# Two key chunks loaded and turned on their own, the rest by a transposed transfer; folds, pools and double-step plans in another order

## The chip, the core and the metric

The kernel runs on one core of a Trainium2 chip. Its time is the device time of one execution in microseconds (us); the median of several executions is what counts. The core has five engines that run side by side, each with its own instruction stream in a fixed order: TensorE (PE, with weight loads PEld), VectorE (DVE), ScalarE (ACT), GpSimd (POOL) and SyncE (SP), which here issues nearly all transfers. Each waits on semaphores for the others. SBUF is the on-chip memory; PSUM holds what TensorE computes, in eight banks here used in pairs.

## What is computed

The input x has 2048 tokens of 640 numbers (bfloat16); there are 32 heads of 20. Two attention layers A and B work on the same x, and a gate per token mixes them.

```python
# A: linear attention, features are softmax(+p) and softmax(-p) of p = (x W) w_phi
qkv = (x @ wqkv).reshape(B, S, 3, H, Dh) ...
pk = jnp.einsum('bhsd,hdf->bhsf', k, w_phi)
phi_k = jnp.concatenate([_softmax(pk), _softmax(-pk)], axis=-1)
kv = jnp.einsum('bhsf,bhsd->bhfd', phi_k, v);  z = jnp.einsum('bhsf->bhf', phi_k)
o = einsum(phi_q, kv) / (einsum(phi_q, z) + 1e-06);  a = o @ wo
# B: four segments of 512 tokens, causal softmax attention and a memory M, z of earlier segments
p = _softmax(q_s k_s^T * scale + mask);  a_dot = p v_s
a_mem = phi(q_s) M / (phi(q_s) z + 1e-06)
o = sig(beta) * a_mem + (1 - sig(beta)) * a_dot;  M += phi(k_s)^T v_s;  z += sum phi(k_s);  b = o @ wo
# mix
g = sigmoid((x * gate_w).sum(-1));  out = g * a + (1 - g) * b
```

## The kernel before, in words

Nearly every instruction's order is written out by hand, engine by engine; no planner reorders it. So an instruction that waits holds up all that stand behind it on its engine, and a transfer that waits holds up SP's queue.

**Front (L84 to L315).** The key weights of layer A are multiplied by w_phi beforehand (the fold), so that one product gives the features' exponents. The five 128-row blocks of these weights (wnat_k) come in five transfers, blocks 0, 2, 4 issued by ACT (L96), 1 and 3 by SP (L105). A step `T`n (`emit_foldT`, L175) turns block n with five TensorE transposes and copies it out of PSUM (L180, to WkT, on DVE or ACT). A step `M`n (`emit_foldM`, L182) makes six small matmuls of it with Wphi, a masked w_phi that DVE and POOL build (L144), and ACT copies the result to WkA (L190). A step `X`n (`emit_xT`, L192) turns 256 tokens of x, loaded plainly into x_nat (L102), with ten transposes, and DVE copies them to the first quarter of xTf (L200). The order is T0 T1 T2 M0 M1 T3 T4 M2 X0 X1 M3 M4 (L305), behind 25 transposes of ident_b that only warm TensorE up (L304). The other quarters of x, 512 tokens each, come turned by the transfer itself (`emit_xturn`, L113): quarters 1 and 2 right after the loads of the value weights WvA (L110), quarter 3 after chunk 1.

**Key chunks (L224 to L257).** The 2048 tokens are handled in 16 chunks of 128. Chunk sc belongs to quarter sc // 4 and takes every fourth token of it (`key_tokens`, L224, through the view xTk); quarter 3 is first put into runs (xP, L116). `emit_a1` (L229) computes pk (ten matmuls with WkA) and pv (ten with WvA); ACT takes two exponentials of pk and copies pv, DVE sums and takes the reciprocal, POOL multiplies (EkSn). `emit_zmove` (L252) sends EkSn to Z with two transfers on SP. The gate column of WvA is filled from gw (L314, L315).

**Rest of layer A (to L682).** The kv products, the sums over Z, the query features (pq), then for each of 16 query chunks the numerators (`emit_num`, L455, in three PSUM pools nps0 to nps2), the denominators and the divisions (tt, L508 on DVE; oA, L666 on POOL). Between them go half projections (320 columns each) of layer B's first segment, out of the pool pps.

**Layer B (L687 on).** 32 steps (segment and group of four heads) are taken in pairs: 16 double steps. Each makes five bursts: TensorE computes two PSUM tiles of scores (st_ps, L736, pools st_a and st_b), ACT takes their exponentials (PT, L740), POOL cuts the triangles (L747). Between the bursts TensorE gets other work, one letter an item, by a string of PLAN per double step:

- `h` half projection of the next segment (five matmuls, L922; DVE copies them out, L928), `o` and `f` out projections (L866; out by L875 or L877, and then a transfer L879). All use the two buffers of the pool bps.
- `k`, `q` an exponential of a projected chunk on ACT (L894); `x`, `y` the two DVE instructions that finish its features (L897, L898), x for keys and y for queries; `z` the transposed transfer of finished query features (L907).
- `A` and `B` products with the values for the double step's first step and for the step before it (L790), `D` and `C` the last of these with the memory products (L798, L803) and the epilogue on DVE and POOL (L815 to L837).
- `t` turns one output chunk (L841), `u` turns the first three column blocks of the last segment's four chunks (L960).

SHARES holds four numbers per double step: after burst n the items are handed out until that share of the plan's matmul work is done, and after the fifth burst all that is left. An `h`, `o` or `f` counts 0.137 for each matmul of 320 columns; k, q, x, y, z, t and u count nothing, so they fall between their neighbours. The tail (L1000 on) finishes the last step and the last four output chunks, which read the turned blocks of `u` (L1046).

Of the kernel before, what the change touches and what calls it, by code (L numbers as in the profile page):

```python
# [15 lines left out]
def kernel(  # L16
# [35 lines left out]
    xq = xTf[:, S // 4:].rearrange("p (g c t) -> p g c t", g=4, c=KC)  # L52
    beta_b = const.tile([P, H], BF16, name="beta_b")
# [27 lines left out]
    x_nat = []  # L81
# [3 lines left out]
    xv = x2.rearrange("(c p) d -> p c d", p=P)  # L85
# [13 lines left out]
    def emit_xload():  # L99
        x_nat.append(xload.tile([P, 2, D], BF16, name="x_nat"))  # L100
        c0 = 2 * len(x_nat) - 2
        nc.sync.dma_start(out=x_nat[-1], in_=xv[:, c0:c0 + 2, :])  # L102

    for c in (1, 3):
        nc.sync.dma_start(out=wnat_k[:, c], in_=wsrc(D)[:, c])  # L105
    for n in range(2):
        emit_xload()
    nc.sync.dma_start(out=gw5, in_=gate_w.rearrange("(c p) -> c p", p=P))
    for bk in range(2):
        nc.sync.dma_start(out=WvA[:, :, bk, 0:320], in_=wsrc(2 * D)[:, :, bk * 320:(bk + 1) * 320])  # L110
# [71 lines left out]
    def emit_foldM(WT, dst, ic):  # L182
        ps = w2tile("fold_ps")
        for n, (j, bk, lo, hi) in enumerate(PIECES):
            h0 = TH[j][0]
            nc.tensor.matmul(ps[:, bk, (lo - 16 * bk) * DH:(hi - 16 * bk) * DH],
                             lhsT=WT[:, j, ic * P:(ic + 1) * P],
                             rhs=Wphi[:, j, lo - h0:hi - h0, :].rearrange("p h d -> p (h d)"),
                             start=(n in FIRST), stop=(n in LAST))
        nc.scalar.copy(out=dst[:, ic, :].rearrange("p (b n) -> p b n", b=2), in_=ps[:, :, 0:320])  # L190

    def emit_xT(n):  # L192
        pair = w2tile("xtp")
        for u in range(2):
            tp = pair[:, u].bitcast(BF16)[:, 0:D].rearrange("p (c t) -> p c t", c=KC)
            for c in range(KC):
                nc.tensor.transpose(out=tp[:, c, :], in_=x_nat[n][:, u, c * P:(c + 1) * P], identity=ident_b)
# [4 lines left out]
    WkT = wq_hold.tile([P, KC, D], BF16, name="WkT")  # L202

# [18 lines left out]
    xTk = xq.rearrange("p g c (m r) -> p g c r m", r=4)  # L222

    def key_tokens(c, sc):  # L224

        g, r = divmod(sc, 4)
        return xTk[:, g, c, r] if g < 3 else xP[:, c, r * P:(r + 1) * P]

    def emit_a1(sc):  # L229
        pk, pv = w2tile("pk"), w2tile("pv")  # L230
        for ps, W, n in ((pk, WkA, 320), (pv, WvA, 321)):
            by_row = [(c, bk) for c in range(KC) for bk in range(2)]
            for c, bk in by_row if sc == 0 else sorted(by_row, key=lambda t: t[1]):
                rhs = WvA[:, c, bk, :] if W is WvA else WkA[:, c, bk * 320:(bk + 1) * 320]
                nc.tensor.matmul(ps[:, bk, 0:n], lhsT=key_tokens(c, sc), rhs=rhs,  # L235
                                 start=(c == 0), stop=(c == KC - 1))
# [65 lines left out]
    warm = [aps.tile([P, KC, P], BF16, name="warm", tag="w2") for _ in range(2)]  # L302
    for n in range(25):
        nc.tensor.transpose(out=warm[n % 2][:, n % KC, :], in_=ident_b, identity=ident_b)  # L304
    for step in ("T0", "T1", "T2", "M0", "M1", "T3", "T4", "M2", "X0", "X1", "M3", "M4"):  # L305
        n = int(step[1])
        if step[0] == "T":
            emit_foldT(wnat_k, WkT, n, nc.scalar.copy if n in (1, 4) else nc.vector.tensor_copy)
        elif step[0] == "M":
            emit_foldM(WkT, WkA, n)  # L310
        else:
            emit_xT(n)
    gw_ps = aps.tile([P, KC], BF16, name="gw_ps", tag="w2")
    nc.tensor.transpose(out=gw_ps, in_=gw5, identity=ident_b[0:KC, 0:KC])  # L314
    nc.vector.tensor_copy(out=WvA[:, :, :, 320:321],  # L315
                          in_=gw_ps[:, :, None, None].to_broadcast([P, KC, 2, 1]))
    for sc in range(NCH):
        emit_a1(sc)
        emit_zmove(sc)
        if sc == 1:  # L320
            emit_xturn(3)
# [239 lines left out]
    for what in "ppppvzppppdvp":  # L561
# [14 lines left out]
    *nps, pps = [nps_stack.enter_context(tc.tile_pool(  # L576
        name=n, bufs=b, space=bass.MemoryType.PSUM, reuse_waits="tile"))
        for n, b in (("nps0", 1), ("nps1", 1), ("nps2", 1), ("pps", 2))]
# [108 lines left out]
    with ExitStack() as bctx:  # L687
# [5 lines left out]
        bps, st_a, bnd, st_b = [bctx.enter_context(tc.tile_pool(  # L693
            name=n, bufs=b, space=bass.MemoryType.PSUM, reuse_waits="tile"))
            for n, b in (("bps", 2), ("st_a", 1), ("bnd", 1), ("st_b", 1))]
# [239 lines left out]
        def half_items(s, order):  # L935
# [207 lines left out]
```

## Time and profile before

| what | us |
|---|---|
| median of three runs | 320.29 (318.81 to 320.96) |
| the profiled execution | 319.04 |
| its span, first to last instruction | 317.3 |
| TensorE busy | 303.7 (96 %) |
| ScalarE busy | 252.8 (80 %) |
| VectorE busy | 225.4 (71 %) |
| GpSimd busy | 209.2 (66 %) |

The granted clock of TensorE was 1.000 over the span.

How to read it: a line of the timeline begins with the start in us from the span's start and the duration, then the engine, the line of the kernel, the operation, the tile written and the tile read, their shapes, and how many such instructions were merged (x9). In square brackets stands how long the engine had been idle before it and who ended that wait. In the chain of work that ended last each row is a start, a duration and what held the end up at that time. A row of a tile or a line gives the shortest, the median and the longest duration in ns. "DMA to landing" is the time from a transfer's issue until its data was there.

### The profile page before, as it was taken

To read this page: it belongs to the slowest core of one execution; us is meant where nothing else is said; L and a number is where in the kernel's file an instruction comes from. 1 tells how busy PE (TensorE), PEld (TensorE's weight loads), DVE (VectorE), ACT (ScalarE), POOL (GpSimd) and SP (SyncE) were. 2 spreads that over 40 slices of the span, in tenths; PEclk is the share of its full clock that TensorE was granted. 3 is DMA by queue.
4 is the path that set the end of the run, shared out by engine and by line. 5 is a ranking of instruction groups with operands and counts; after the bars stand their busy time and mean duration, and the time that the engine had idled before them with its cause. 6 is when DMAs were issued, how large, how long until landed. Compare 5 with 4: busy or idle time off the path is not lost.

```text
span 317.3 us, 9775 instructions
## 1 busy us (share of the span) xinstructions
PE 303.7 (96%) x4024; PEld 209.2 (66%) x4024; DVE 225.4 (71%) x505; ACT 252.8 (80%) x321; POOL 209.2 (66%) x308
## 2 busy tenths in 40 slices
PE   7999999999999999789999999999999999999995
PEld 7788877855578888356655566665656666656673
DVE  3477897998779997857668587778655864454463
ACT  5677888367846648799999899999989898898953
POOL 8588599103247989855656667778787777756550
PEclk9999999999999999999999999999999999999999
DMA  7949844439127989744331353473654443222132
GB/s 215 223 111 203 200 110 128 129 99 366 56 19 136 127 122 150 138 79 70 69 68 33 68 108 70 89 109 61 102 98 89 87 90 66 75 71 58 48 89 83
DMA packets 91814, 34.22 MB, mean 108 GB/s; under 512 B 79866, under 2 KB 91770, under 8 KB 91770
## 3 DMA queue, kind: packets, MB, share of 16 engines
q1 hardware_dynamic: 91194, 32.95, 49.3%
q10 hardware_dynamic: 576, 0.66, 0.8%
q8 instruction: 31, 0.51, 0.7%
q14 instruction: 13, 0.11, 0.1%
HBM read 6.42 MB, written 2.62 MB: 29 GB/s over the span
## 4 chain that ended last, share of the span: by engine, by line
PE 69%; ACT 21%; DVE 2%; issue 2%; DMA 2%; POOL 2%; SPq 1%; ACTq 0%; DVEq 0%; POOLq 0%
ACT PT L740 19%; PE st_ps L736 9%; PE proj L922 9%; PE proj L866 9%; PE pk L235 7%; PE pq L402 7%; PE pv L235 7%; PE nda L790 6%; PE proj L538 5%; PE num L460 3%; DMA x_nat<-in_A_x_dram 2%; PE kv_ps L375 2%; PE num L477 1%; DVE tt L508 1%; POOL oA L666 1%
## 5 line engine op out<-in xcount | busy, mean ns | idle before, releaser
L740 ACT ACTIVATE PT<-st_ps 128x1024 bf16<-128x1024 f32 x160 | 153.5, 1023 | 14.7 <-PE st_ps L736 12.7
L747 POOL TENSOR_SCALAR_AFFINE_SELECT PT<-PT 128x512 bf16<-128x512 bf16 (+1 forms) x130 | 87.0, 688 | 48.7 <-ACT PT L740 48.6
L790 PEld LDWEIGHTS <-PT 128*128 128x128 bf16 x1280 | 40.4, 96 | 9.6 <-issue 5.8
L790 PE MATMUL nda<-vB,PT 128*128 128x21 bf16 x1240 | 41.9, 173 | 0.1
L247 POOL TENSOR_TENSOR EkSn<-Ek,krec 128x1280 bf16<-128x1280 bf16 x15 | 35.1, 2360 | 8.8 <-DVE krec L246 8.1
L922 PEld LDWEIGHTS <-xTf 128*128 128x128 bf16 x300 | 26.4, 97 | 16.1 <-issue 7.7
L928 DVE CAST Z<-proj 128x320 bf16<-128x320 f32 x44 | 21.0, 488 | 21.3 <-PE proj L922 21.3
L235 PEld LDWEIGHTS <-xTf 128*128 128x128 bf16 x240 | 27.1, 113 | 5.8
L409 ACT ACTIVATE Eq<-pq 128x1024 bf16<-128x1024 f32 x20 | 19.4, 1021 | 12.3 <-PE pq L402 12.3
L243 DVE TENSOR_REDUCE ksum<-Ek 128x64 f32<-128x1280 bf16 x16 | 23.6, 1475 | 7.6 <-ACT Ek L239 7.4
L866 PE MATMUL proj<-WkA,oTA 128*128 128x320 bf16 x160 | 28.2, 300 | 0.0
L508 DVE TENSOR_TENSOR tt<-num,rr 128x640 f32<-128x640 f32 x32 | 25.0, 813 | 4.5 <-POOL rr L501 1.7
L239 ACT ACTIVATE Ek<-pk 128x640 bf16<-128x640 f32 x32 | 20.8, 702 | 9.2 <-PE pk L235 8.2
L666 POOL TENSOR_TENSOR oA<-tt 128x640 bf16<-128x640 f32 x16 | 24.7, 1550 | 5.2 <-DVE tt L508 5.0
L736 PE MATMUL st_ps<-Z 32*128 32x384 bf16 (+3 forms) x256 | 24.0, 299 | 3.9 <-ACT PT L740 3.3
L736 PE MATMUL st_ps<-Eq 32*128 32x512 bf16 (+3 forms) x256 | 24.7, 299 | 2.4 <-ACT PT L740 1.9
L402 PE MATMUL pq<-xTf,WqA 128*128 128x512 bf16 x100 | 22.2, 379 | 0.0
L830 POOL TENSOR_TENSOR oB<-td 128x320 bf16<-128x320 f32 x22 | 19.0, 863 | 4.1 <-DVE td L827 4.1
L866 PE MATMUL proj<-WvA,oT 128*128 128x320 bf16 x120 | 21.3, 300 | 0.0
L827 DVE TENSOR_TENSOR td<-nda,rec 128x640 f32<-128x640 f32 x23 | 19.0, 825 | 2.1
L922 PE MATMUL proj<-WqB,xTf 128*128 128x320 bf16 x110 | 17.8, 300 | 1.8 <-DVE Z L928 1.8
L538 PEld LDWEIGHTS <-xTf 128*128 128x128 bf16 x180 | 16.2, 97 | 4.6
(177 smaller groups left out, 548.6 us busy)
## 6 DMA issues: line engine op xcount, KB each, us to landing
Z<-EkSn SPq DMA_DIRECT2D x32, 160.0 KB, 2.8
out_dram<-orow SPq DMA_DIRECT2D x8, 160.0 KB, 1.8
out_dram<-oTA SPq DMA_DIRECT2D x6, 160.0 KB, 1.9
WvA<-in_A_wqkv_dram SPq DMA_DIRECT2D x2, 400.0 KB, 6.7
WvB<-in_B_wv_dram SPq DMA_DIRECT2D x1, 800.0 KB
WkB<-in_B_wk_dram SPq DMA_DIRECT2D x1, 800.0 KB, 6.7
WqB<-in_B_wq_dram SPq DMA_DIRECT2D x1, 800.0 KB, 8.4
WkA<-in_A_wo_dram SPq DMA_DIRECT2D x1, 800.0 KB, 10.1
```

The costliest lines, as they stand in the source:

```text
L235: nc.tensor.matmul(ps[:, bk, 0:n], lhsT=key_tokens(c, sc), rhs=rhs, start=(c == 0), stop=(c == KC - 1))
L247: (nc.vector if sc == NCH - 1 else nc.gpsimd).tensor_tensor(out=EkSn[:, sc].rearrange("p s (h f) -> p (s h) f", f=DH), in0=Ek.rearrange("p ...
L402: nc.tensor.matmul(pq[:, half, :], lhsT=WqA[:, c, j * P:(j + 1) * P], rhs=xq[:, 2 * qb + half, c], start=(c == 0), stop=(c == KC - 1))
L508: nc.vector.tensor_tensor(out=tt[:, sgn].rearrange("p (b h) d -> p b h d", b=2), in0=ps, in1=csb, op=ALU.mult)
L538: nc.tensor.matmul(ps, lhsT=xq[:, sc // 4, cc, sc % 4 * P:(sc % 4 + 1) * P], rhs=W[:, cc, half * 320:(half + 1) * 320], start=(cc == 0), s ...
L666: nc.gpsimd.tensor_tensor(out=oA.rearrange("p (h d) -> p h d", d=DH), in0=tt[:, 0], in1=tt[:, 1], op=ALU.add)
L736: nc.tensor.matmul(ps[:, i - i0, o:o + L - c * P], lhsT=kT[32 * i:32 * i + 32, c * P:(c + 1) * P], rhs=qT[32 * i:32 * i + 32, c * P:L], st ...
L740: nc.scalar.activation(out=PT[:, i0:i0 + 2], in_=ps, func=ACT.Exp, scale=SCALE_B)
L747: nc.gpsimd.affine_select(out=v, in_=v, pattern=[[0, n_i], [1, P]], compare_op=ALU.is_ge, fill=0.0, base=0, channel_multiplier=-1)
L790: nc.tensor.matmul(nd[:, j, i], lhsT=block(st, c)[:, i, (j - c) * P:(j - c + 1) * P], rhs=vB[:, c, 4 * st.g + i, :], start=(c == 0), stop= ...
L866: nc.tensor.matmul(ps, lhsT=oT[:, k % KC], rhs=W[:, k % KC, hs], start=(k == 0), stop=(k == n - 1))
L922: nc.tensor.matmul(ps, lhsT=xq[:, sc // 4, k, sc % 4 * P:(sc % 4 + 1) * P], rhs=W[:, k, half * 320:(half + 1) * 320], start=(k == 0), stop ...
```

## The change

Front. Of the first quarter of x only 256 tokens are still loaded plainly: the rows 4m and 4m + 1, two neighbouring rows to each partition. They are just the tokens of chunks 0 and 1. One step X0 turns them, and DVE copies the two chunks one by one to the first half of xP. The whole first quarter comes by a transposed transfer too, the first of three that now stand behind the WvA loads; quarter 3 again follows the Z moves of chunk 1. So chunks 0 and 1 read xP, chunks 2 to 11 the turned quarters, 12 to 15 xP. The warm-up multiplies zeros, which DVE sets, and no longer waits for ident_b. The order of the steps becomes T0 T2 M0 T1 M2 T4 M1 T3 X0 M4 M3; T0 and all five M are copied out by ACT ("a"), T1 to T4 by DVE ("d"). The first key product sums over the blocks in the order 0, 2, 1, 4, 3. The products of chunks 0 and 1 are issued as k0, g (the gate column), k1, v0, v1, and then the rest of both chunks.

Later. The PSUM pools of the second part of layer A and those of layer B are opened in another order, so that they lie on other banks; the numerators use nps0, nps1, nps2 in turn. In the plans of the double steps 0, 3, 12, 14 and 15 items change places, and some SHARES change by 0.01 to 0.03.

```diff
-    for n in range(2):
-        emit_xload()
...
+        elif what[0] == "x":
+            x_nat[n] = xload.tile([P, 2, D], BF16, name="x_nat")
+            nc.sync.dma_start(out=x_nat[n], in_=x2[0:512].rearrange("(m r) d -> m r d", r=4)[:, 2 * n:2 * n + 2])
...
-    emit_xturn(1)
-    emit_xturn(2)
+    for g in range(3):
+        emit_xturn(g)
...
+    zero_b = xload.tile([P, P], BF16, name="zero_b")
+    nc.vector.memset(zero_b, 0.0)
...
     def emit_xT(n):
...
-        dst = xq[:, 0, :, 2 * n * P:2 * (n + 1) * P].rearrange("p c (u t) -> p u c t", u=2)
-        src = pair.bitcast(BF16)[:, :, 0:D].rearrange("p u (c t) -> p u c t", c=KC)
-        nc.vector.tensor_copy(out=dst, in_=src)
+        for u in range(2):
+            nc.vector.tensor_copy(out=xP[:, :, (2 * n + u) * P:(2 * n + u + 1) * P], in_=tps[u])
...
-        return xTk[:, g, c, r] if g < 3 else xP[:, c, r * P:(r + 1) * P]
+        return xTk[:, g, c, r] if 2 <= sc < 12 else xP[:, c, r * P:(r + 1) * P]
...
-        nc.tensor.transpose(out=warm[n % 2][:, n % KC, :], in_=ident_b, identity=ident_b)
-    for step in ("T0", "T1", "T2", "M0", "M1", "T3", "T4", "M2", "X0", "X1", "M3", "M4"):
+        nc.tensor.matmul(warm[n % 2][:, 0, 0:P], lhsT=zero_b, rhs=zero_b, start=True, stop=True)
+    for step in "T0a T2d M0a T1d M2a T4d M1a T3d X0 M4a M3a k0 g k1 v0 v1 r0 r1".split():
...
-        t = nps[(0, 2, 1)[(2 * ch + sgn) % 3]].tile([P, 2, 512], F32, name="num")
+        t = nps[(2 * ch + sgn) % 3].tile([P, 2, 512], F32, name="num")
...
-        for n, b in (("nps0", 1), ("nps1", 1), ("nps2", 1), ("pps", 2))]
+        for n in ('nps2', 'pps', 'nps0', 'nps1')}
...
-            for n, b in (("bps", 2), ("st_a", 1), ("bnd", 1), ("st_b", 1))]
+            for n in ('st_a', 'st_b', 'bps', 'bnd')}
...
-        PLAN = ("qyhhhhozkxooAD", "qhhBhyChkzoxAooD", "qhhBhyChkzoxAooD",
-                "ooBqoyoCokzoxADo", "hkhBhhChhqyhADztt", "khhBhxhqChfhyzAD",
+        PLAN = ("qhhhhyzokxooAD", "qhhBhyChkzoxAooD", "qhhBhyChkzoxAooD",
+                "ooBqoyoCokzxoADo", "hkhBhhChhqyhADztt", "khhBhxhqChfhyzAD",
...
-                "fBfCffADt", "fBftCfftAD", "fBftCffADf", "fuBfCfAfDf")
+                "fBfCfftAD", "fBftCfftAD", "fBtfCffADf", "fBfCufAffD")
-        SHARES = [[0.2, 0.42, 0.55, 0.77], [0.19, 0.4, 0.6, 0.85], [0.21, 0.4, 0.6, 0.8], [0.19, 0.4, 0.6, 0.81], [0.19, 0.41, 0.58, 0.8], [0.19, 0.41, 0.63, 0.86], [0.2, 0.4, 0.6, 0.83], [0.2, 0.4, 0.6, 0.83], [0.2, 0.4, 0.6, 0.8], [0.23, 0.4, 0.6, 0.82], [0.2, 0.4, 0.6, 0.82], [0.21, 0.4, 0.6, 0.82], [0.2, 0.4, 0.59, 0.8], [0.2, 0.39, 0.6, 0.8], [0.19, 0.4, 0.59, 0.8], [0.2, 0.4, 0.6, 0.85]]
+        SHARES = [[0.2, 0.42, 0.55, 0.77], [0.19, 0.4, 0.6, 0.85], [0.19, 0.4, 0.6, 0.8], [0.19, 0.4, 0.61, 0.79], [0.19, 0.38, 0.58, 0.8], [0.19, 0.41, 0.63, 0.86], [0.2, 0.4, 0.6, 0.83], [0.2, 0.4, 0.6, 0.83], [0.2, 0.4, 0.6, 0.8], [0.23, 0.39, 0.6, 0.82], [0.2, 0.39, 0.6, 0.82], [0.21, 0.39, 0.6, 0.82], [0.2, 0.4, 0.59, 0.8], [0.21, 0.39, 0.6, 0.8], [0.19, 0.37, 0.59, 0.81], [0.2, 0.41, 0.6, 0.85]]
```

More of the change, by code (lines that the diff above doesn't have):

```diff
@@ L97 @@
     nc.sync.dma_start(out=Wc, in_=A_w_phi.rearrange("h f g -> (h f) g").rearrange("(c p) g -> p c g", p=P))
[L99 to L105, printed above, removed]
-    for n in range(2):
-        emit_xload()
-    nc.sync.dma_start(out=gw5, in_=gate_w.rearrange("(c p) -> c p", p=P))
-    for bk in range(2):
-        nc.sync.dma_start(out=WvA[:, :, bk, 0:320], in_=wsrc(2 * D)[:, :, bk * 320:(bk + 1) * 320])
+    for what in "w1 w3 x0 g v0 v1".split():
+        n = int(what[1:]) if len(what) > 1 else 0
+        if what[0] == "w":
+            nc.sync.dma_start(out=wnat_k[:, n], in_=wsrc(D)[:, n])
+        elif what[0] == "x":
+            x_nat[n] = xload.tile([P, 2, D], BF16, name="x_nat")
+            nc.sync.dma_start(out=x_nat[n], in_=x2[0:512].rearrange("(m r) d -> m r d", r=4)[:, 2 * n:2 * n + 2])
+        elif what[0] == "g":
+            nc.sync.dma_start(out=gw5, in_=gate_w.rearrange("(c p) -> c p", p=P))
+        else:
+            nc.sync.dma_start(out=WvA[:, :, n, 0:320], in_=wsrc(2 * D)[:, :, n * 320:(n + 1) * 320])
     def emit_xturn(g):
@@ L300, in emit_beta @@
         return omgh_b, CM
-    warm = [aps.tile([P, KC, P], BF16, name="warm", tag="w2") for _ in range(2)]
+    warm = [w2tile("warm") for _ in range(2)]
     for n in range(25):
-        nc.tensor.transpose(out=warm[n % 2][:, n % KC, :], in_=ident_b, identity=ident_b)
-    for step in ("T0", "T1", "T2", "M0", "M1", "T3", "T4", "M2", "X0", "X1", "M3", "M4"):
-        n = int(step[1])
+        nc.tensor.matmul(warm[n % 2][:, 0, 0:P], lhsT=zero_b, rhs=zero_b, start=True, stop=True)
+    for step in "T0a T2d M0a T1d M2a T4d M1a T3d X0 M4a M3a k0 g k1 v0 v1 r0 r1".split():
+        n = int(step[1:2] or 0)
         if step[0] == "T":
-            emit_foldT(wnat_k, WkT, n, nc.scalar.copy if n in (1, 4) else nc.vector.tensor_copy)
+            emit_foldT(wnat_k, WkT, n, {"a": nc.scalar.copy, "d": nc.vector.tensor_copy}[step[2]])
         elif step[0] == "M":
-            emit_foldM(WkT, WkA, n)
-        else:
[L312 to L317, printed above, removed]
+            emit_foldM(WkT, WkA, n, {"a": nc.scalar.copy, "d": nc.vector.tensor_copy}[step[2]])
+        elif step[0] == "X":
+            emit_xT(n)
+        elif step[0] == "k":
+            emit_a1_mm(n, pks, WkA, 320)
+        elif step[0] == "v":
+            emit_a1_mm(n, pvs, WvA, 321)
+        elif step[0] == "r":
+            emit_a1(n)
+            emit_zmove(n)
+        else:
+            emit_gw()
+    emit_xturn(3)
+    for sc in range(2, NCH):
         emit_a1(sc)
         emit_zmove(sc)
-        if sc == 1:
-            emit_xturn(3)
         if 8 <= sc < 12:
@@ L575 @@
     nps_stack = ExitStack()
-    *nps, pps = [nps_stack.enter_context(tc.tile_pool(
-        name=n, bufs=b, space=bass.MemoryType.PSUM, reuse_waits="tile"))
-        for n, b in (("nps0", 1), ("nps1", 1), ("nps2", 1), ("pps", 2))]
+    num_pools = {n: nps_stack.enter_context(tc.tile_pool(
+        name=n, bufs=2 if n == "pps" else 1, space=bass.MemoryType.PSUM, reuse_waits="tile"))
+        for n in ('nps2', 'pps', 'nps0', 'nps1')}
+    nps, pps = [num_pools[f"nps{n}"] for n in range(3)], num_pools["pps"]
     oTA = resB.tile([P, NCH + 1, KC, P], BF16, name="oTA")
```

43 lines of the change are left out of this document (27 added, 16 removed).

## The prediction

> **What bounds the kernel now.** I read the page first, then the busy time by stretch, then the chain of work that ended last, and last the timeline at the places where that chain leaves TensorE. The page gives the span; the profiled execution took 319.04 us, so 1.74 us lie around the span. The three runs shown have a median of 320.29, 1.25 above this execution.
>
> ```profile
> span 317.3 us, 9775 instructions
> ```
>
> ```profile
> 0.00:10.20 10.20, 8.26 (x101) 7.22 (x101) 4.26 (x7) 5.22 (x8) 8.39 (x33) 1.00 0.90 234
> 10.20:89.50 79.30, 79.21 (x837) 56.93 (x838) 65.45 (x180) 56.79 (x81) 43.28 (x37) 1.00 0.59 154
> 127.50:135.90 8.40, 5.80 (x47) 2.81 (x47) 6.17 (x8) 6.25 (x9) 6.11 (x6) 1.00 0.71 138
> 135.90:175.00 39.10, 36.95 (x553) 23.15 (x552) 27.92 (x68) 37.50 (x43) 23.66 (x44) 1.00 0.34 63
> 175.00:305.00 130.00, 126.54 (x1923) 81.22 (x1917) 82.13 (x180) 119.05 (x129) 93.66 (x156) 1.00 0.41 82
> ```
>
> Each row is a stretch, its length, and the busy time (and count) of PE, its weight loads, DVE, ACT and POOL in it; at its end the granted clock, the DMA engines' share and GB/s. From 10.2 to 89.5 TensorE is busy 79.21 of 79.30 us: there a change gains only what it starts earlier. From 135.9 to 175 ScalarE is the fuller engine (37.50 of 39.10), from 175 to 305 TensorE (126.54 of 130, all its idle time 3.46 us). Two stretches are limited by neither: the first 10.2 us, with the DMA engines 0.90 busy, and 127.5 to 135.9, where TensorE is busy 5.80 and ScalarE 6.25 of 8.40 us. The change touches both. The chain at the start:
>
> ```profile
> 2.83 5.69 DMA x_nat<-in_A_x_dram
> 8.56 0.73 PE xtp L197 x10
> 9.29 0.80 PE fold_ps L186 x12
> 10.09 0.12 PE gw_ps L314
> 10.21 1.55 PE pk L235 x10
> ```
>
> ```profile
> 15.97 1.36 PE pk L235 x10
> 17.33 1.37 PE pv L235 x10
> ```
>
> The second load of x, landing at 8.52, holds the last turn, the last two folds and the first key product. The second fence is the same chain at chunk 2.
>
> **The front, part by part.** The second x load goes, with its ten turns and one copy. What remains is a chain through the engines, so I lay it out with these rows.
>
> ```profile
> 1.43 2.85 PE L304 MATMUL warm<-ident_b 128*128 128x128 bf16 x25 [1.43 <-POOL tiny L127]
> 3.71 1.54 POOL L144 TENSOR_TENSOR Wphi<-Wc,wmask 128x140 bf16<-128x140 bf16 x3 [0.42 <-DMA Wc<-in_A_w_phi_dram]
> 3.97 0.42 PEld L178 LDWEIGHTS <-wnat_k 128*128 128x128 bf16 x5
> 5.13 0.69 ACT L180 COPY WkT<-wtp 128x640 bf16<-128x640 bf16 x1 [1.40 <-PE wtp L178]
> 5.42 1.03 PE L186 MATMUL fold_ps<-Wphi,WkT 128*128 128x240 bf16 x12
> 6.58 0.73 PE L178 MATMUL wtp<-ident_b,wnat_k 128*128 128x128 bf16 x10
> 7.57 0.56 PEld L197 LDWEIGHTS <-x_nat 128*128 128x128 bf16 x10
> ```
>
> T0 starts at 3.97 as before. Its copy now is ScalarE's, 0.69 us, ready near 5.2; Wphi's last part is POOL's at 5.25. So M0 starts near 5.25, and TensorE then goes on almost without a gap: a fold is about 0.5 us (twelve matmuls in 1.03), a T of five turns about 0.35 (ten in 0.73). After M0: T1 to 6.15, M2 to 6.65, T4 to 7.0, M1 to 7.5, T3 to 7.9. The weight rows have landed by then (ten turns of T3 and T4 ran from 6.58), and so has the first x load (its turns began at 7.57); I leave that instant as it is, though the new load takes two rows in one piece. X0 ends near 8.6, M4 and M3 near 9.6. k0 starts there instead of at 10.21, and the order 0, 2, 1, 4, 3 of its sums asks for M3's copy last. The gate column's 0.12 us moves behind k0. So the key products begin their steady run (10.09 - 9.6) about 0.5 us earlier. Ends: 0, if a copy on the way waits as long as the load did; 1.0, the distance of the two x loads (8.52 less 7.57), which is all the load itself could free.
>
> Warm-up matmuls take zeros from VectorE instead of ident_b from POOL, and could start before 1.43. T0 waits for its data until 3.97 anyway, and 25 x 0.11 us end by then: 0 on the path. Removed turns and copies beside it: counted already, since TensorE waits no more. Splitting X0's copy in two, and giving T0, M-steps and T4 other engines: in the layout above.
>
> [...]
>
> **What now waits for the transposed transfer.** Chunk 2 and 3 are now read from a transfer that wasn't there; in front of it stands one x load less.
>
> ```profile
> 4.79 10.25 SPq L113 DMA_TRANSPOSE xTf<-in_A_x_dram  x2
> L113 SPq DMA_TRANSPOSE xTf<-in_A_x_dram x1: 6673/6673/6673, 4.8 to 4.8; - x1
> DMA to landing us min/median/max: 10.2/10.2/10.2
> 17.74 4.01 SPq L255 DMA_DIRECT2D Z<-EkSn  x4
> ```
>
> The second and third line are for the first of the two: issued at 4.79 behind the WvA loads, it held SP for 6.67 us and landed 10.2 us after its issue, at 15.0. Now the first is issued about 0.45 us earlier (one issue less) and behind 320 KB less: 14 to 14.5. Chunk 2's first product comes after k0, g, k1, v0, v1: 15.97 - 0.5 = 15.5. So it is hidden by about 1 us; if that cover is gone, every us of lateness costs one. The second transfer follows by about 3.6 us (10.25 - 6.67) and is needed two chunks later (2 x 2.73 us), the third four chunks after that. SP is held by one such transfer more, 3.6 us, and is free near 18 (4.3 + 10.25 + 3.6). beta and the Z moves stand behind it. The first Z move was issued at 17.74, so it slips by under 1 us. xturn(3) still follows the second chunk's moves, which wait for POOL, and the sums over Z come after all sixteen chunks. Cost 0.
>
> **The first double step.** This is the large term.
>
> ```profile
> 127.97 1.94 ACT L740 ACTIVATE PT<-st_ps 128x1024 bf16<-128x1024 f32 x2
> 128.12 3.12 POOL L666 TENSOR_TENSOR oA<-tt 128x640 bf16<-128x640 f32 x2
> 128.37 1.48 DVE L897 TENSOR_SCALAR Eq<-Eq 128x640 bf16<-128x640 bf16 x1
> 128.45 1.40 PE L922 MATMUL proj<-WkB,xTf 128*128 128x320 bf16 x9
> 129.88 2.04 DVE L898 SCALAR_TENSOR_TENSOR Eq<-Z,Eq 128x640 bf16<-128x640 bf16 x1
> 130.21 1.94 ACT L740 ACTIVATE PT<-st_ps 128x1024 bf16<-128x1024 f32 x2 [0.29 <-PE st_ps L736]
> 131.20 2.41 POOL L747 TENSOR_SCALAR_AFFINE_SELECT PT<-PT 128x512 bf16<-128x512 bf16 x3
> 131.84 0.88 DVE L928 CAST Z<-proj 128x320 bf16<-128x320 f32 x2
> 132.37 1.25 PE L922 MATMUL proj<-WqB,xTf 128*128 128x320 bf16 x8 [1.77 <-DVE Z L928]
> 133.99 3.77 ACT L740 ACTIVATE PT<-st_ps 128x1024 bf16<-128x1024 f32 x4 [1.84 <-PE st_ps L736]
> ```
>
> ```profile
> L897 DVE TENSOR_SCALAR ek<-ek x18: 316/318/811, 144.3 to 260.4; 128x640 bf16<-128x640 bf16 x18
> L898 DVE SCALAR_TENSOR_TENSOR Eq<-Z,ek x11: 824/826/1205, 144.7 to 260.8; 128x640 bf16<-128x640 bf16 x11
> ```
>
> The item y (L897 and L898) stands ahead of the four half projections. It takes VectorE from 128.37 to 131.9; both projection buffers are full, nobody copies them out, TensorE waits 1.77 us, and ScalarE behind it 1.84. In the new plan the four copies stand ahead of y. In the old clock: pieces come at 0.137 us (nine in 1.40, the last 0.3). Halves 1 and 2 are done near 129.2 and 130.5, each copied 0.5 us later, in time for halves 3 and 4. The third burst, after the 18th piece, is computed at 131.6, its second half when ScalarE leaves its tile at 132.2. ScalarE goes on at 132.15 instead of 133.99: **1.84 us**. Then y: half 4 is copied by 133.3, y takes 0.32 + 0.82 to 134.5 at best. The out projections' first buffer is wanted again by their third, near 135.2, when ScalarE has work until 136.05. So y costs nothing there if it is done by about 135.2, and up to 1.2 us if it is as slow as before (1.48 + 2.04). Why it was slow is in the rows: it ended with POOL's two oA instructions (131.24). At its new place POOL has only its selects, 0.8 us each, and later such pairs have medians of 0.32 and 0.82. I take 1.8; ends 0.6 and 1.85. The turn z, now straight behind y, stands behind the same two turns on SP, and its rows are read only in the next segment.
>
> [...]
>
> **Later plans, shares and pools.** One bank is renumbered for another: the last num tiles are succeeded by the same pools in the same order, and the first three num tiles follow tiles that were read out before them. Cost 0, hidden by a TensorE that is busy with pq until they are wanted; 0.7 us, one copy, if not. In the last steps the oT turns stand a little earlier and the four turns of oB later.
>
> ```profile
> 297.86 5.31 SPq L960 DMA_TRANSPOSE oTA<-oB  x4
> 299.39 0.49 DVE L875 TENSOR_TENSOR oTA<-proj,oTA 128x320 bf16<-128x320 f32 x1 [1.31 <-PE proj L866]
> 305.88 0.98 PE L1046 MATMUL st_ps<-WvA,oTA 128*128 128x320 bf16 x6
> oTA<-oB SPq DMA_TRANSPOSE x4, 2.4
> ```
>
> They now stand behind one more output, whose source (L875) was ready at 299.9: issued 300.3 to 305.6, the first landing near 302.7, the last near 306.7. The tail reads the first at 305.9 and the last some 4 us later: hidden, by 3 us. The moved shares (0.01 to 0.03 of a step's items, some 6.5 us by the 0.137 us of a piece) shift a burst by 0.1 to 0.2 us each. Where TensorE is the bound all idle time is 3.46 us over 130, so the sum can be anything from -1 to +1; I take a gain of 0.1.
>
> **Sum.** 0.5 + 1.8 + 0.1 = 2.4: from 319.04 to 316.6 for such an execution, and from the median of 320.29 to **317.9**. A difference of about 1% is what a measurement of this kernel can tell from no change; 2.4 is 0.75%.
>
> **Rivals.** (a) The wait of y is only moved: the out projections stall for 1.2 us; 0.5 + 0.6 + 0.1 = 1.2, so 319.1. For it: y's two slow rows; against: its neighbours from then on. (b) The later plans take out stalls: the 3.46 us contain about 1 to win; 316.9 or less. (c) Slower, by the first transposed transfer: chunk 2 stands still until it lands. From a landing at 15.5 on it costs; at 17.9 (15.5 + 2.4) all is given back, and at 21.1 the kernel is 1% slower. 10.2 us from issue was the longest such row, so this needs over 3 us more. (d) Slower a little, by the later plans: each of a dozen bursts 0.25 us too early or too late, 3 us, 320.9. (e) The change doesn't do what it says in the first step: ScalarE finds no work at 132.15 for another reason; 0.6 gained, 319.7.
>
> **How the numbers follow.** Forecast 0.58, (a) 0.14, (b) 0.12, (c) 0.04, (d) 0.07, (e) 0.05. The range goes from the ends of the terms with the runs' own scatter of about a us: 320.29 - 1.0 - 1.85 - 1.0 is 316.4, and runs lie up to 0.7 below, so 315.7; above, (a) and (e) are inside and (d) is not: 320.4. Faster by over 1% means under 317.1: most of (b) and some 0.28 of the forecast, together 0.26. Slower by over 1% (over 323.5): (c) and little else, 0.04. The rest, 0.70, within 1%.
>
> **What would show it.** Right: k0 at 9.4 to 9.8 and chunk 2's k near 15.5 without a DMA wait; in the first double step no wait of TensorE for L928, and ScalarE's idle time there under 0.5; L897 and L898 near 0.3 and 0.8 after the four copies; from 136 to the end the same lengths within a us. Wrong: TensorE waiting for xTf at chunk 2; a wait for L877 in the first step; new idle time of ScalarE past 140; the tail waiting for the turns of oB.

## The result and the profile after

The changed kernel takes 315.83 us (median of six executions, 315.41 to 316.12), the kernel before 319.90 (six, 318.81 to 320.96). The ratio is 0.9875 with a 95% interval of 0.9851 to 0.9899: 1.25% faster. The medians lie 4.1 us apart where 2.4 were forecast. The profiled executions took 315.77 and 319.04, with spans of 314.1 and 317.3: between these two only 3.3 us are gone, 3.2 of them in the span. So there are two questions: where the 3.2 come from, and why the medians differ by 0.8 more than the profiled executions. One execution of the kernel before took 934.53 us and is left out of everything below.

Busy time by stretch in the kernel after, cut as in the prediction (the last cuts 3 us earlier, with the end); columns as there.

```profile
0.00:10.20 10.20, 8.82 (x98) 7.90 (x99) 4.20 (x9) 5.53 (x8) 8.39 (x33) 1.00 0.89 209
10.20:89.50 79.30, 79.23 (x846) 56.49 (x845) 66.16 (x181) 56.92 (x81) 44.32 (x40) 1.00 0.62 161
127.50:135.90 8.40, 8.00 (x91) 4.33 (x88) 5.34 (x11) 8.10 (x10) 6.97 (x8) 1.00 0.78 149
175.00:302.00 127.00, 123.95 (x1861) 79.28 (x1860) 81.37 (x178) 116.33 (x127) 91.54 (x152) 1.00 0.45 81
```

The stretch of the first double step is filled: TensorE 8.00 of 8.40 us where it had 5.80, ScalarE 8.10 where it had 6.25. In the first 10.2 us TensorE has 0.56 more. The rest reads as before.

The chain of work that ended last, at the start:

```profile
1.75 4.88 DMA wnat_k<-in_A_wqkv_dram
6.68 0.45 PE wtp L179 x5
7.13 0.40 PE fold_ps L187 x6
7.53 0.28 PE wtp L179 x5
7.81 0.64 PE xtp L198 x10
8.44 0.80 PE fold_ps L187 x12
9.24 1.41 PE pk L240 x10
14.96 1.36 PE pk L240 x10
```

No load of x holds the chain any more; one weight block does, until 6.63, and from there TensorE goes on without a wait. The first key product starts at 9.24 instead of 10.21, chunk 2's at 14.96 instead of 15.97, with no wait for its transfer. (The timeline has the two at 9.07 and 14.79, since a matmul's row begins there before the one ahead of it has ended.) This is how the transfers stand in the timeline (SP's queue; the second fence is the row of the first transposed transfer alone):

```profile
4.34 13.57 SPq L112 DMA_TRANSPOSE xTf<-in_A_x_dram  x3
17.95 0.58 SPq L120 DMA_DIRECT2D beta_b<-in_B_beta_dram  x1
18.65 2.68 SPq L267 DMA_DIRECT2D Z<-EkSn  x4
```

```profile
L112 SPq DMA_TRANSPOSE xTf<-in_A_x_dram x1: 6249/6249/6249, 4.3 to 4.3; - x1
DMA to landing us min/median/max: 10.0/10.0/10.0
```

The first one lands at 4.34 + 10.0 = 14.3; SP is free at 17.91.

The timeline of the first double step:

```profile
126.75 1.94 ACT L758 ACTIVATE PT<-st_ps 128x1024 bf16<-128x1024 f32 x2
128.98 5.68 ACT L758 ACTIVATE PT<-st_ps 128x1024 bf16<-128x1024 f32 x6 [0.30 <-PE st_ps L754]
129.21 1.32 PE L940 MATMUL proj<-WqB,xTf 128*128 128x320 bf16 x8
131.78 0.49 DVE L946 CAST Z<-proj 128x320 bf16<-128x320 f32 x1 [1.20 <-PE proj L940]
132.19 0.32 DVE L915 TENSOR_SCALAR Eq<-Eq 128x640 bf16<-128x640 bf16 x1
132.54 0.83 DVE L916 SCALAR_TENSOR_TENSOR Eq<-Z,Eq 128x640 bf16<-128x640 bf16 x1
135.16 3.78 ACT L758 ACTIVATE PT<-st_ps 128x1024 bf16<-128x1024 f32 x4
```

ScalarE's second to fourth burst are one row of six without a gap. y (now L915 and L916) stands behind the fourth copy and takes 0.32 and 0.83 us where it took 1.48 and 2.04. The burst behind it starts at 135.16; in the kernel before it started at 138.26.

Where the time went is read best from the start of three bursts of exponentials: the first of the first double step, the one just named, and the last that is in all of them.

| kernel | first burst | after the step | last burst | gain before, in, behind the step |
|---|---|---|---|---|
| before | 127.97 | 138.26 | 304.59 | |
| after | 126.75 | 135.16 | 301.41 | 1.22, 1.88, 0.08 |
| e1, plan of the first double step alone | 127.61 | 136.03 | 302.35 | 0.36, 1.87, 0.01 |
| e2, all but the plans | 127.30 | 137.60 | 303.92 | 0.67, -0.01, 0.01 |
| e3, after with the old later plans | 126.89 | 135.30 | 301.64 | 1.08, 1.88, -0.01 |
| e4, before with less beside y | 128.00 | 136.41 | 302.74 | -0.03, 1.88, 0.00 |

Of the 1.22 us ahead of the step, 1.01 are there at chunk 2. The other 0.2 come at the kv products: 250 matmuls that both kernels have alike begin at 56.18 and are followed at 61.97 in before, 55.17 and 60.73 in after. These took 5.79 and 5.56 us there, 5.57 in e1, 5.80 in e2 and 6.05 in e3, with the same code; so this is scatter.

### The profile page after: what moved, and what is told of

Its sections match the earlier page's. It is cut to its first block, busy times and chain, and to the rows that moved or that the text cites. A ratio compares the mean times of both kernels' runs of the same rounds, so it can differ in the third digit from the quotient of the medians.

```text
span 314.1 us, 9759 instructions
## 1 busy us (share of the span) xinstructions
PE 304.0 (97%) x4014; PEld 208.3 (66%) x4014; DVE 223.7 (71%) x507; ACT 252.2 (80%) x320; POOL 209.0 (67%) x308
## 4 chain that ended last, share of the span: by engine, by line
PE 73%; ACT 22%; DMA 2%; issue 1%; DVE 1%; ACTq 0%; DVEq 0%
ACT PT L758 19%; PE st_ps L754 9%; PE proj L884 9%; PE proj L940 9%; PE pk L240 7%; PE pq L418 7%; PE proj L554 7%; PE pv L240 7%; PE nda L808 6%; PE num L476 4%; PE kv_ps L391 2%; DMA wnat_k<-in_A_wqkv_dram 2%; PE num L493 1%; PE nda L816 1%; ACT ek L912 1%
## 5 line engine op out<-in xcount | busy, mean ns | idle before, releaser
L940 PEld LDWEIGHTS <-xTf 128*128 128x128 bf16 x300 | 26.4, 97 | 14.2 <-issue 5.7
L754 PE MATMUL st_ps<-Z 32*128 32x512 bf16 (+3 forms) x256 | 24.7, 299 | 3.2 <-ACT PT L758 2.3
L240 PEld LDWEIGHTS <-xTf 128*128 128x128 bf16 x200 | 22.6, 113 | 4.7
L554 PEld LDWEIGHTS <-xTf 128*128 128x128 bf16 x180 | 16.2, 97 | 4.6
L884 PEld LDWEIGHTS <-oTA 128*128 128x128 bf16 x160 | 13.6, 97 | 8.0 <-issue 4.0
```

Source lines behind the costliest of these rows:

```text
L554: nc.tensor.matmul(ps, lhsT=xq[:, sc // 4, cc, sc % 4 * P:(sc % 4 + 1) * P], rhs=W[:, cc, half * 320:(half + 1) * 320], start=(cc == 0), s ...
L754: nc.tensor.matmul(ps[:, i - i0, o:o + L - c * P], lhsT=kT[32 * i:32 * i + 32, c * P:(c + 1) * P], rhs=qT[32 * i:32 * i + 32, c * P:L], st ...
L884: nc.tensor.matmul(ps, lhsT=oT[:, k % KC], rhs=W[:, k % KC, hs], start=(k == 0), stop=(k == n - 1))
L940: nc.tensor.matmul(ps, lhsT=xq[:, sc // 4, k, sc % 4 * P:(sc % 4 + 1) * P], rhs=W[:, k, half * 320:(half + 1) * 320], start=(k == 0), stop ...
```

## The experiments

Ratios are to executions of the kernel before on the same chip: median 319.98 for e1 to e4, 319.34 for e5 to e8, 319.6 for e9.

**e1: the first plan alone**, in the kernel before.

```diff
-        PLAN = ("qyhhhhozkxooAD", "qhhBhyChkzoxAooD", "qhhBhyChkzoxAooD",
+        PLAN = ("qhhhhyzokxooAD", "qhhBhyChkzoxAooD", "qhhBhyChkzoxAooD",
```

> The kernel before, with the first double step's plan alone changed (y behind the four half projections). Theory: the 1.88 us that separate the two traces between the first burst and the fourth come from y's place, so this one string is worth about 1.9 us: ScalarE goes on at the third burst without its 1.84 us of idle time, and the median falls by 1.9 (0.6 %). Rival: the gain needs the earlier front or the other banks of layer B as well; then under 0.5 us.

316.94 us, ratio 0.9902 (0.9882 to 0.9922). The span is 315.1, so 2.2 below the profiled execution of before, but the medians lie 3.0 apart. The timeline of the step:

```profile
129.85 5.67 ACT L740 ACTIVATE PT<-st_ps 128x1024 bf16<-128x1024 f32 x6 [0.30 <-PE st_ps L736]
```

The wait of 1.84 us is gone and nothing stands in its place; 1.87 us stay to the end. The other 0.36 came ahead of the step, where the code is that of before, so it is scatter.

**e2: everything but the plans** (front and pools new, PLAN and SHARES old; the shares are cut after the fourth double step).

```diff
-        PLAN = ("qhhhhyzokxooAD", "qhhBhyChkzoxAooD", "qhhBhyChkzoxAooD",
...
+        PLAN = ("qyhhhhozkxooAD", "qhhBhyChkzoxAooD", "qhhBhyChkzoxAooD",
...
-        SHARES = [[0.2, 0.42, 0.55, 0.77], [0.19, 0.4, 0.6, 0.85], [0.19, 0.4, 0.6, 0.8], [0.19, 0.4, 0.61, 0.79],
...
+        SHARES = [[0.2, 0.42, 0.55, 0.77], [0.19, 0.4, 0.6, 0.85], [0.21, 0.4, 0.6, 0.8], [0.19, 0.4, 0.6, 0.81],
...
```

> The changed kernel with all the old plans and shares: the front and the pools' order alone. Theory: chunk 2 starts 1.0 us earlier than before and the sum of A keeps 1.2 us, so the first scores' exponentials begin near 126.8 and the median falls by 1.0 to 1.3. The 1.84 us of ScalarE's idle time in the first double step are back. Rival: the plans were what made room, and the front's us is lost again in layer B; then under 0.5.

318.37 us, ratio 0.9944 (0.9924 to 0.9963). The wait is back, as long as in before:

```profile
133.33 3.77 ACT L758 ACTIVATE PT<-st_ps 128x1024 bf16<-128x1024 f32 x4 [1.85 <-PE st_ps L754]
```

The front is worth 0.67 us in this execution, where after has 1.0 at chunk 2.

**e3: the changed kernel with the later plans and shares of before**, so that only the first plan is new.

```diff
-                "ooBqoyoCokzxoADo", "hkhBhhChhqyhADztt", "khhBhxhqChfhyzAD",
+                "ooBqoyoCokzxoADo", "hkhBhhChhqyhADztt", "khhBhxhqChfhyzAD",
...
-                "fBfCfftAD", "fBftCfftAD", "fBtfCffADf", "fBfCufAffD")
...
+                "fBfCffADt", "fBftCfftAD", "fBftCffADf", "fuBfCfAfDf")
...
```

> The changed kernel with the old plans of the double steps 3, 12, 14 and 15 and all the old shares; only the first plan stays new. Theory: the later plans and shares are worth nothing that shows (the two traces are 3.1 to 3.3 us apart at every burst from the fourth to the last), so within 0.3 us of the changed kernel, ratio to before 0.987 to 0.989. Rival: the new plans take out stalls in some executions, and the median gains by them what the two profiled executions don't show (4.1 us in the medians against 3.2 in the spans); then 0.8 us slower than the changed kernel.

316.26 us, ratio 0.9880 (0.9858 to 0.9902), which the interval of after includes. From the burst after the step to the last one it takes 0.09 us longer than after, and within 0.02 as long as before, e1, e2 and e4. The later plans are worth 0.1.

**e4: y undisturbed.** Is y slow in before by itself, or by GpSimd beside it? Here y stays at its old place, and the last two of GpSimd's additions (oA) are left out.

```diff
-        oA = a3w.tile([P, D], BF16, name="oA", bufs=4)
-        nc.gpsimd.tensor_tensor(out=oA.rearrange("p (h d) -> p h d", d=DH),
-                                in0=tt[:, 0], in1=tt[:, 1], op=ALU.add)
+        if ch < NCH - 2:
+            oA = a3w.tile([P, D], BF16, name="oA", bufs=4)
+            nc.gpsimd.tensor_tensor(out=oA.rearrange("p (h d) -> p h d", d=DH),
+                                    in0=tt[:, 0], in1=tt[:, 1], op=ALU.add)
```

> The kernel before, in which POOL's last two additions oA are left out and the transfers of chunks 14 and 15 take the addition of chunk 13 once more; the output of two chunks is not the reference's. y keeps its old place. Theory: the two y instructions were slow because POOL's oA instructions run beside them; without these they take 0.32 and 0.83 us, VectorE is free at 129.6 instead of 131.9, the first half projection is copied 0.4 us late, TensorE's wait of 1.77 us goes, and the span falls by about 1.8 us though y was not moved. Rival: they are slow for another reason (their place right after the division, the data's home); then 1.48 and 2.04 us remain and the span with them.

317.27 us, ratio 0.9917 (0.9898 to 0.9937). The step's timeline:

```profile
128.41 0.32 DVE L898 TENSOR_SCALAR Eq<-Eq 128x640 bf16<-128x640 bf16 x1
128.76 0.83 DVE L899 SCALAR_TENSOR_TENSOR Eq<-Z,Eq 128x640 bf16<-128x640 bf16 x1
130.23 5.68 ACT L741 ACTIVATE PT<-st_ps 128x1024 bf16<-128x1024 f32 x6 [0.30 <-PE st_ps L737]
```

y takes 1.15 us instead of 3.52, and the step gains the same 1.88. So y was not too early in the order; it was beside oA. Moving it behind the copies or taking oA away gains the same in the step.

**e5: the old order of the folds** (T0 T1 T2 M0 M1 T3 T4 M2 X0 M3 M4, with the same single load of x).

```diff
-    for step in "T0a T2d M0a T1d M2a T4d M1a T3d X0 M4a M3a k0 g k1 v0 v1 r0 r1".split():
+    for step in "T0d T1a T2d M0a M1a T3d T4a M2a X0 M3a M4a k0 g k1 v0 v1 r0 r1".split():
```

> The changed kernel with the folds in the order and on the engines of before (T0 T1 T2 M0 M1 T3 T4 M2 X0 M3 M4); one x load, k0 g k1 v0 v1 and all else as changed. Theory: the front gains because the second x load is gone from the chain, and the order of the folds is worth little: k0 near 9.1 to 9.4, the median within 0.3 us of the changed kernel (ratio to before 0.987 to 0.989). Rival: half of the front's us comes from folding in the order of landing; then k0 near 9.8 and 0.5 us slower than the changed kernel.

316.28 us, ratio 0.9894 (0.9871 to 0.9918); its profiled execution has a span of 314.0, that of after 314.1. Chunk 2 starts at 14.77 in the timeline, in after at 14.79. One wait is new, 0.16 us inside k0 for M4's copy, which the start of k0 at 8.78 makes good. The order is worth nothing that shows. That leaves the load that went as the source of the front's gain; this is by elimination, since no run puts the load back alone.

**e6: the first quarter's transfer second.** Is chunk 2's transfer hidden, and by how much?

```diff
-    for g in range(3):
+    for g in (1, 0, 2):
```

> The changed kernel with the transposed transfers issued in the order 1, 0, 2, so that the quarter that chunk 2 reads comes second. In the changed kernel the second landed at 17.5 (10.6 and 6.9 us) and chunk 2 began at 14.8. Theory: TensorE waits for the landing, as nothing else is in its order: chunk 2 at about 17.5, 2.7 us of idle time, and all of it stays to the end; median 2.4 to 2.8 us above the changed kernel, about 0.996 of before. Rival: the chunks behind it have slack enough, and under 1 us is left at the end.

318.35 us, ratio 0.9981 (0.9957 to 1.0004). The chunk's row, and then the granted clock (third column from the end) behind it in half microseconds:

```profile
17.14 1.70 PE L240 MATMUL pk<-WkA,xTf 128*128 128x320 bf16 x10 [2.28 <-DMA xTf<-in_A_x_dram]
```

```profile
17.50:18.00 0.50, 0.50 (x6) 0.41 (x5) 0.03 (x1) 0.00 (x0) 0.33 (x1) 1.00 1.28 291
18.00:18.50 0.50, 0.50 (x6) 0.43 (x4) 0.00 (x0) 0.00 (x0) 0.50 (x1) 0.89 1.27 289
18.50:19.00 0.50, 0.50 (x4) 0.27 (x3) 0.00 (x0) 0.12 (x1) 0.50 (x1) 0.50 0.80 173
21.50:22.00 0.50, 0.50 (x5) 0.30 (x3) 0.47 (x2) 0.44 (x1) 0.00 (x0) 0.70 0.81 233
22.00:22.50 0.50, 0.50 (x5) 0.42 (x4) 0.28 (x1) 0.25 (x1) 0.08 (x1) 1.00 0.95 202
```

The transfer is late by 2.28 us and that is paid one for one, as forecast of a cover that is gone. But this execution took 320.26, 4.5 above after. Behind the wait the clock is at half speed for some 3.4 us, and half of that, 1.7 us, is what it costs by an estimate. Of ten executions four show a mean clock of 0.994 to 0.995 (spans 317.9 to 318.5), six 0.999 to 1.000 (316.1 to 316.7, which is after and the wait alone). So a wait of TensorE can cost more than its own length, which bears on the 0.8 us.

**e7: the old warm-up**, 25 turns of ident_b.

```diff
...
-        nc.tensor.matmul(warm[n % 2][:, 0, 0:P], lhsT=zero_b, rhs=zero_b, start=True, stop=True)
+        nc.tensor.transpose(out=warm[n % 2][:, n % KC, :], in_=ident_b, identity=ident_b)
```

> The changed kernel with the old warm-up: 25 turns of ident_b behind POOL instead of 25 matmuls of zeros. Theory: nothing beyond the scatter of the clock's opening, which moved k0 between 8.8 and 9.4 in three executions of the same front; median within 0.3 us of the changed kernel. [...]

316.32 us, ratio 0.9892 (0.9870 to 0.9914). The first fold and the first key product:

```profile
5.59 0.57 PE L185 MATMUL fold_ps<-Wphi,WkT 128*128 128x240 bf16 x6 [0.43 <-ACT WkT L179]
9.08 1.11 PE L238 MATMUL pk<-WkA,xP 128*128 128x320 bf16 x7
```

The fold that follows nothing but turns is as quick as any later one (0.56), and k0 starts within 0.01 us of after's. In the trace's record of the clock full speed begins at 4.84, ahead of the first fold. The kind of the warm-up makes no difference here.

**e8: the numerators' pools opened and used as before.**

```diff
-        t = nps[(2 * ch + sgn) % 3].tile([P, 2, 512], F32, name="num")
+        t = nps[(0, 2, 1)[(2 * ch + sgn) % 3]].tile([P, 2, 512], F32, name="num")
...
-        for n in ('nps2', 'pps', 'nps0', 'nps1')}
...
+        for n, b in (("nps0", 1), ("nps1", 1), ("nps2", 1), ("pps", 2))]
```

> The changed kernel with the pools nps0, nps1, nps2, pps opened in the old order and used in the old turn. The front makes one PSUM tile less, so that order now puts the first numerator on the banks of the last pq, whose two exponentials end 2.2 us after the numerator could start. Theory: TensorE stops for these 2.2 us near 88, where it is the fuller engine, and the kernel is 1.5 to 2.2 us slower than the changed one: the new order of the pools is no gain but a repair that the front needs, and my cost of 0 for the edit held only for the new order. Rival: the work behind it is limited by VectorE and POOL, and less than 0.5 us is left at the end.

319.12 us, ratio 0.9975 (0.9950 to 0.9999). A wait is new at the first numerators, which in after follow the last pq at 88.15 without one:

```profile
91.06 0.96 PE L476 MATMUL num<-kvn,Eq 128*128 128x240 bf16 x12 [2.03 <-ACT Eq L425]
```

```profile
92.00:92.50 0.50, 0.50 (x5) 0.27 (x3) 0.50 (x2) 0.00 (x0) 0.00 (x0) 0.52 0.00 0
95.00:95.50 0.50, 0.50 (x11) 0.50 (x10) 0.00 (x0) 0.02 (x1) 0.00 (x0) 0.57 0.00 0
```

The new front takes one PSUM tile fewer, and so with the old order the first numerator falls on the banks of the last pq, which ScalarE is still reading. The new order of the pools belongs to the front: it mends what the front would have cost. Again half of the executions, six of twelve, show the clock at 0.995 (spans 317.9 to 318.8), the others 315.9 to 316.9.

**e9: the gap filled.** In the kernel before, 11 matmuls into a bank that nobody reads are put into the wait of the first double step. They are added work and shorten nothing.

```diff
-        PLAN = ("qyhhhhozkxooAD", "qhhBhyChkzoxAooD", "qhhBhyChkzoxAooD",
+        PLAN = ("qyhhwhhozkxooAD", "qhhBhyChkzoxAooD", "qhhBhyChkzoxAooD",
...
+                elif w == "w":
+                    items += [(0.0, lambda: nc.tensor.matmul(nda[:, 0, 0:320], lhsT=ident_b, rhs=WkB[:, 0, 0:320],
+                                                             start=True, stop=True)) for _ in range(11)]
```

> The kernel before, with eleven matmuls more in the first double step: TensorE multiplies ident_b by 320 columns of WkB, into a part of PSUM that nothing reads, between the second and the third half projection, where it waits 1.77 us for the copies. y stays where it was, so the wait of ScalarE (1.84 us) stays too. Theory: the executions of before come in two kinds, mean granted clock 0.993 to 0.995 (span 318.1 to 319.5) and 0.998 to 1.000 (316.8 to 317.9), because this wait sometimes halves the clock for some 3.4 us afterwards, as it does behind a wait of 2.3 us in the kernel with the quarters exchanged. With the gap filled every execution has a clock of 0.998 or more, spans stay at 316.8 to 318, the upper kind is gone and the median falls by 0.3 to 0.9 us though work was added. Rival: the clock falls for another reason; then about half the executions stay at 0.995.

319.10 us, ratio 0.9983 (0.9966 to 1.0000). ScalarE's wait is as long as ever, but TensorE's is 0.30:

```profile
130.15 1.66 PE L982 MATMUL nda<-WkB,ident_b 128*128 128x320 bf16 x11
132.11 1.25 PE L922 MATMUL proj<-WqB,xTf 128*128 128x320 bf16 x8 [0.30 <-DVE Z L928]
133.72 3.77 ACT L740 ACTIVATE PT<-st_ps 128x1024 bf16<-128x1024 f32 x4 [1.86 <-PE st_ps L736]
```

All twelve executions have a mean clock of 0.998 to 1.000 and spans of 317.1 to 318.1. The medians lie 0.5 us apart in favour of the kernel with more work; the interval just reaches 1, so the kinds of execution tell it better than the ratio.

**e10 and e11: the kernel before twice more**, unchanged, for a profile of the other kind.

> The kernel before, unchanged, for another look. Theory: with about one chance in two its mean clock is 0.993 to 0.995; then the granted clock is 0.5 in a stretch of some 3 us that begins after the wait in the first double step (near 132), and the later bursts come 1 to 1.5 us later than in the look shown. Rival: the lower clock lies at another place, such as the front.

> The kernel before, unchanged, for one more look, so that at least one of the two is likely to be of the lower clock. Theory and rival as for the other look: the clock at 0.5 behind the wait near 132, or somewhere else.

e11 (319.07 us, span 317.4) is as the profile first shown. e10 (320.10, span 318.4, mean clock 0.995) is the other kind:

```profile
132.14 2.29 PE L922 MATMUL proj<-WqB,xTf 128*128 128x320 bf16 x8 [1.79 <-DVE Z L928]
135.01 3.77 ACT L740 ACTIVATE PT<-st_ps 128x1024 bf16<-128x1024 f32 x4 [3.12 <-PE st_ps L736]
```

```profile
131.50:132.00 0.50, 0.00 (x0) 0.00 (x0) 0.50 (x2) 0.40 (x1) 0.50 (x1) 1.00 0.97 190
132.00:132.50 0.50, 0.36 (x2) 0.24 (x2) 0.48 (x2) 0.00 (x0) 0.50 (x2) 0.52 0.04 7
135.00:135.50 0.50, 0.50 (x3) 0.27 (x4) 0.00 (x0) 0.49 (x1) 0.00 (x0) 0.57 0.24 46
135.50:136.00 0.50, 0.50 (x5) 0.23 (x3) 0.37 (x1) 0.50 (x2) 0.00 (x0) 1.00 0.00 0
```

The wait is the same 1.8 us. But the eight matmuls behind it take 2.29 us instead of 1.25, and ScalarE gets its next burst after 3.12 us instead of 1.84.

## Why the prediction was right where it was, and where it was not

**The first double step: right, 1.88 measured for 1.8.** The mechanism is shown from both sides: y moved (e1), and what slows y taken away (e4), give 1.87 and 1.88, each alone. y itself was over at 133.37; in the times of the kernel before, 1.22 us later at the first burst, that is 134.6, as forecast (134.5). So rival (a), the wait only moved, did not happen: there is no wait for the out projections' copies. Beside oA the two instructions took 1.48 and 2.04 us, without it 0.32 and 0.83 (e4). At the new place GpSimd had only selects: one ended at 132.21, 0.02 us after y's first instruction had begun, and the next began at 132.89, 0.35 us into the second instruction, which took its 0.83. At other places of the kernel after, the same two instructions are longer beside a select. Each row here is one instruction:

```profile
132.89 0.96 POOL L765 TENSOR_SCALAR_AFFINE_SELECT PT<-PT 128x512 bf16<-128x512 bf16 x1 [0.69 <-ACT PT L758]
133.81 0.63 POOL L765 TENSOR_SCALAR_AFFINE_SELECT PT<-PT 128x512 bf16<-128x512 bf16 x1
133.96 0.67 DVE L915 TENSOR_SCALAR Z<-Z 128x640 bf16<-128x640 bf16 x1
141.47 0.64 POOL L765 TENSOR_SCALAR_AFFINE_SELECT PT<-PT 128x512 bf16<-128x512 bf16 x1 [1.82 <-ACT PT L758]
141.57 1.20 DVE L916 SCALAR_TENSOR_TENSOR Eq<-Z,ek 128x640 bf16<-128x640 bf16 x1
```

Where the select began first, VectorE's instruction is longer (0.67 for 0.32, 1.20 for 0.83); where y's second instruction began first, at 132.54, the select is (0.96 for 0.63). So y was quick at its new place, where no select from before ran on beside it; that selects don't matter is not what it shows.

**The front: right in kind, 1.0 for 0.5.** The step that was too large is "a fold is about 0.5 us, a T about 0.35". It divided rows of the timeline, which reach into the step behind them: in after a fold alone has a row of 0.56 there and a T one of 0.44, while in the chain, where one step's end lies under the next, a fold alone is 0.40 and a T 0.28. Over five M and the four T behind the first that is 0.78 us (5 x 0.10 and 4 x 0.07); the wait for a weight block, until 6.63, took part of it again. So k0 came at 9.07, ahead of the 9.4 to 9.8 that were to show the forecast right.

Also, the gain varies. Three executions with the same front start k0 at 8.77 (e3), 9.07 (after) and 9.41 (e2), and differ in when TensorE reaches its full pace: the fold at 5.2 takes 0.57, 0.71 and 0.95 us. The code is the same, and the trace's record of the clock says what differs: full speed begins at 4.24 in e3 and only at 6.91 in e2 (the trace of after has no entry). In e6 and e8 it goes the same way: 4.74 with a first fold of 0.57 and k0 at 8.97, and 6.68 with 0.95 and 9.34. What sets that instant isn't shown. In before it began at 4.16 in the first profile and at 5.72 in e10, the first fold at 5.42 and 5.74, but k0 at 10.21 and 10.22: with the second load of x in the chain, the difference was gone by then. e5 and e7 show that neither the order of the folds nor the kind of the warm-up carries the gain.

**The transfers: hidden, as forecast, with half the margin.** Landing at 14.3 was in the range given; chunk 2 comes at 14.8 instead of 15.5, so 0.5 us are left and not 1. Rival (c) is what e6 made happen: 2.28 us late, 2.3 us later at the end where the clock held.

**The banks: 0, as forecast, but only for the new order.** "0.7 us, one copy, if not" was the price of a wrong order; e8 shows 2.0 and the clock on top of it. That the first numerators follow tiles read out before holds for the new order alone, so it was no mere renumbering.

**Later plans: 0.08 for 0.1**, and the turns of oB cost nothing: they are issued from 297.11, and no wait of the tail is put down to them. Rivals (b) and (d), stalls taken out or put in by these plans, did not happen; (e) neither.

**What was not seen: 0.8 us of the medians.** The step that failed is the sum's last one, "from the median of 320.29 to 317.9": it took the 1.25 us between the profiled execution and the median as scatter that both kernels have. The runs put it down to the wait that the change removes. In about half of the executions of before that the experiments ran beside theirs, 24 of 50, the mean clock is 0.993 to 0.995, and on each chip these take 0.8 to 1.3 us more on average than the others. The profile shown was of the upper kind, with the higher clock. e10, of the lower, shows where: the clock is halved for 3.4 us from the end of TensorE's wait for y on. e9 shows that the wait is the cause: with the gap filled and all else as slow as before, the lower kind is gone in twelve of twelve. e1, e4 and after, where the wait is gone by other means, have no clock under 0.998 in 5, 6 and 6 executions, nor have e3, e5 and e7 in 5, 6 and 6; e2, where it stays, has one of 6 at 0.995; e6 and e8, which open another gap, have 4 of 10 and 6 of 12. It also fits the scatter: 318.8 to 321.0 before, 315.4 to 316.1 after. One execution of the other 26 took 321.51 at a clock of 1.000, so the clock is not all of the scatter.

How much of this a median shows depends on how many executions of before are of the lower kind. Beside 8 of 11 of them, the medians of e1, e3 and e4 gain 0.8 to 0.9 more than the profiled executions; beside 9 of 23, those of e5 and e7 gain -0.2 and 0.2 more. Of the six executions of before in the result only the profiled one has its clock on record (1.000), but three of them took 318.8 to 319.6, as the upper kind does, and three 320.2 to 321.0, as the lower. So the 0.8 is put down to the clock by these runs, and not read off the six.

So the 317.9 missed 315.83 by 2.1 us: 0.5 in the front, 0.2 at the kv products, 0.1 in the step, 0.1 behind the last burst, 0.8 put down to the clock, and 0.4 because six executions of before have a median of 319.90 and not 320.29. That 315.83 still lies in the range given, 0.1 above its lower end, is partly luck: the range had 1.0 us for the later plans, which brought 0.1, and the clock, which was in no term, took that place. It is also a time that rival (b) names, but not by its mechanism; and to be faster by over 1%, as it was, had been given 0.26 against 0.70 for within 1%. What stays open is what makes the kv products take 5.56 in one execution and 6.05 in another.

## What to carry to other kernels

A wait of TensorE can cost more than its length (in e10 a wait of 1.79 us, with eight matmuls behind it that took 2.29 us instead of 1.25): look at the mean clock of every execution, not only of the profiled one, and count what the wait does to the clock behind it. If an instruction takes several times its usual duration (y's first took 1.48 us instead of 0.32), look at what the neighbouring engine had begun just before it, and only then move it or its neighbours; here either remedy gave the whole gain. And when a front drops a tile, follow the banks to the next stage: the succession of pools is part of the change (a wait of 2.03 us in e8).

## What the runs showed of the hardware

- Gaps of 1.8 to 2.3 us on TensorE (1.79 in e10, 2.03 in e8, 2.28 in e6) can halve its clock afterwards. In e10 the half microseconds with 0.52 and 0.57 put the slow stretch from 132.02 to 135.43, in e8 the same two values from 92.02 to 95.43, and in e6 0.89 and 0.70 put it from 18.39 to 21.80: 3.41 us each time. It begins 0.1 us before the gap's end in e10 and 0.9 to 1.3 us behind it in the other two. By the record of the clock in these traces that is 126.30 us after full speed first began in e10, 85.34 in e8 and 13.65 in e6, and divided by 37, 25 and 4 each of them gives 3.41 again. In the first profile of before, a gap of 1.77 us at the same place as e10's left the clock at 1.00. What decides isn't shown.
- VectorE's two feature instructions on 128x640 bf16 took 1.48 and 2.04 us beside GpSimd's f32 additions (before) and 0.32 and 0.83 without them (e4). Beside a select that had begun before them they took 0.67 and 1.20; where VectorE began first it took 0.83, and the select 0.96 instead of 0.63 (after).
- A transposed transfer of 512 rows of 640 held SP's queue for 6.25 us where it stood behind other loads and landed 10.0 us after its issue (after).
